# Later squares of the gate weights and a later read of the spread maxima in an attention and GLU kernel

## The chip, the cores and the metric

The kernel runs on one core of one Trainium2 chip. The metric is device time of one execution in microseconds, as the median of the runs shown. TensorE (PE, with its weight loads as PEld), VectorE (DVE), ScalarE (ACT), GpSimd (POOL) and SyncE (SP) work side by side and wait for each other through semaphores. Nearly all transfers are issued by SyncE, in the order in which they are written.

## The reference

A block with a layer norm, sliding-window attention and a gated bilinear feed-forward network, all in float32:

```python
x = A_x                                   # 1 x 2048 x 576
xn = _layernorm(x, axis=-1)
s = _A_ref(xn, A_wqkv, A_wo)              # 32 heads of 18, window 256, softmax
g = _silu(_B_ref(xn, B_w_gate, B_w_up, B_w_down))   # ((xn Wg) * (xn Wu)) Wd, F = 4608
return x + s * g
```

## The kernel before

Every float32 operand is split into two float16 halves, a high and a low one, and a product is made of three float16 matmuls. Weights are first scaled by a power of two, which needs a bound on the size of each weight block.

A prologue normalizes and transposes `x` and projects it to queries, keys and values, which go to DRAM. Then the main loop runs over 72 slots (`NSLOT = NG * NCH`, 18 groups of 256 hidden columns by 4 pieces of the work). One slot makes seven products of the feed-forward network (P1 to P7, a Strassen-like scheme, `prod`) into the PSUM banks `up` and `pv`, and eight accumulations of the down projection (`down`, banks `dn` and `s`). Beside it runs one attention step out of 64, that is two heads and 512 queries: scores into the banks `s` (`score_pairs`), mask and maximum on VectorE (`score`, L982), exponentials on ScalarE (`probs`, L987 and L989), the cast to float16 (`probs_hi`, L994), the low halves on GpSimd (`turn_probs`, L1003), a transposing DMA (L1006), and the product with the values (`weigh`, L1015). Each step has four such rounds, i = 0 to 3.

What the next group needs is made ready one to three slots ahead:

- `ffn_raw` loads the raw weights of gate, up and down.
- `ffn_amax` (L511) takes sums of squares of them on ScalarE, six calls for a group, the last two on the two halves of the gate weights. Its discarded elementwise output goes to the buffer of the tile `spread`, and the sums to `am`.
- `ffn_spread_out` adds the two halves on GpSimd (L515) and writes `am`, 128 x 3 numbers, to DRAM (`sd_f`, L148).
- `ffn_spread_in` reads `sd_f` back so that each partition holds the sums of all 128 (`spread`, L152, 192 KB).
- `ffn_scale` takes their maximum on VectorE (L523) and forms the scales in five tiny instructions on VectorE (L137 to L142) and three on GpSimd (L525 to L527).

The order on each engine comes from one table of times, `W`: `at(slot, t, f, ...)` enters each piece of work at `slot * 18.65 + t`, the list is sorted by that number, and the pieces are issued in that order. Engines then run in order and wait only for data and buffers. The entries of this change are entered with slot `b - 3`, `b` being the first slot of the group, so a time above 18.65 falls in the slot after:

```python
for n in range(6):
    at(b - 3, W["amax"][n], ffn_amax, g, (1, 1, 2, 2, 0, 0)[n], n % 2)
at(b - 3, W["so"], ffn_spread_out, g)
at(b - 3, W["si"], ffn_spread_in, g)
at(b - 2, W["scale"], ffn_scale, g)
```

Neighbours in that slot, on the same scale: the first round's exponentials at 0.77, its cast at 1.85, its low halves and transposition at 2.85, the copy-out `ca1` of product P1 (`copy_out`, L412) at 2.16, the second round's exponentials at 2.98 and its transposition at 5.07, the key loads of the next step at 4.98, its query loads (L952, L953) at 9.2, and `ffn_scale` at 14.98.

Of the kernel before, what the change touches and what calls it, by code (L numbers as in the profile page):

```python
# [20 lines left out]
def kernel(  # L21
# [23 lines left out]
    scale = DH ** -0.5  # L45
# [1003 lines left out]

    NSLOT = NG * NCH  # L1050
    T = 18.65
    W = {"ttr": [-1.39, -1.33, 0.83, 1.5, 8.88, 9.07, 9.1, 9.53], "exp": [0.77, 2.98, 9.73, 10.74], "cast": [1.85, 4.76, 10.51, 10.85], "plo": [2.85, 5.07, 12.24, 14.56], "fin": 5.65, "whi": [7.64, 14.18, 6.44, 16.68], "wlo": [9.45, 16.18, 10.42, 17.34], "dhi": 12.29, "dlo": 17.87, "dlow": 18.11, "sum0": [15.33, 16.23, 24.54], "sum1": [-13.0, 2.34, 7.21], "amax": [12.28, 6.38, 14.78, 15.38, 18.5, 19.95], "scale": 14.98, "hhi0": 18.35, "hlo0": 22.24, "hhi1": 24.39, "hlo1": 26.95, "h1": 18.74, "pv": [17.46, 3.55], "raw0": 10.11, "so": 20.77, "si": 26.88, "pe": {"P5a": 1.05, "P6": 4.39, "P2": 6.57, "P5b": 3.5, "P7": 8.18, "P4": 14.91, "P3": 12.3}, "dn": [1.65, 5.32, 10.61, 10.7, 12.29, 12.31, 16.97, 17.89], "ev": {"ca1": 2.16, "ca2": 6.15, "ca3": 9.47, "add1": 12.5, "add3": 12.36, "t0": 17.27, "add2": 16.63}, "ons": [2, 3, 4, 7], "ld": {"k": 4.98, "q": 9.2, "v": 1.72, "raw1": 1.11, "raw2": 2.66}}
    todo = []

    def at(slot, t, f, *a):
        todo.append((slot * T + t, len(todo), f, a))

    first_slot = 1
    for s in range(NSTEP):
        b = first_slot + s  # L1060
        at(b - 1, W["ld"]["k"], load_k, s)
        at(b - 1, W["ld"]["q"], load_q, s)
        at(b, W["ld"]["v"], load_v, s)
        at(b - 1, 16.6, score_pairs, s, 0)
        at(b, 7.1, score_pairs, s, 2)
        for n in range(8):
            i, j = divmod(n, 2)
            at(b, W["ttr"][n], score, s, i, j)
        for i in range(4):
            at(b, W["exp"][i], probs, s, i)  # L1070
            at(b, W["cast"][i], probs_hi, s, i)
            at(b, W["plo"][i], turn_probs, s, i)
# [272 lines left out]
```

## Time and profile before

| | us |
|---|---|
| median of 3 runs (1571.2 to 1572.65) | 1571.51 |
| profiled execution | 1569.04 |
| its span, first to last instruction | 1567.3 |
| VectorE, all waits for the read of the spread maxima (L523) | 4.3 |
| ScalarE, all squares (L511), 108 calls | 76.8 |

A profile's timeline has a row for each instruction or merged run of instructions: start, duration, engine, line, operation, tiles written and read, shapes, count, and in brackets the idle time of the engine just before it with what ended it. Times count from the start of the span. The waits view sums those idle times by the waiting and the releasing line. A row of the windows view gives, for a stretch, its length, each engine's busy time, the granted clock of TensorE, the mean busy share of the 16 DMA engines and the GB/s moved.

### The profile page before, as it was taken

What the parts mean: (1) busy time and instruction counts of PE and PEld (TensorE: products, weight loads), DVE (VectorE), ACT (ScalarE), POOL (GpSimd) and SP (SyncE); (2) the same over time, 40 slices, a digit from 0 to 9 for tenths busy, and PEclk for the clock granted to TensorE, in tenths of its full rate; (3) what the DMA queues carried; (4) which work ended last, traced back from release to release, by engine and by line L of the source; (5) the groups of instructions that cost most, each with busy time, mean ns of one, the idle gap of its engine ahead of it and who ended that gap; (6) DMA issues with size and microseconds to landing.
All of it is one profiled execution on the core that took longest, in us unless ns stands there. A gap on an engine that the chain in (4) does not pass through costs nothing. (4 is left out here: it accounts for less than half of the span.)

```text
span 1567.3 us, 32521 instructions
## 1 busy us (share of the span) xinstructions
PE 1545.7 (99%) x11857; PEld 890.9 (57%) x11857; DVE 1264.7 (81%) x2914; ACT 1022.1 (65%) x1987; POOL 852.2 (54%) x860
## 2 busy tenths in 40 slices
PE   8999999999999999999999999999999999999998
PEld 5454445555555555555555555555555555555577
DVE  7768678777788989898989888888989898957554
ACT  6547587676767777777777776767777777733230
POOL 3344365646465757576666666575757575822100
PEclk9999999999999999999999999999999999999999
DMA  9593366565748586867777677758686758540435
GB/s 235 165 237 114 113 126 134 103 134 89 143 81 165 109 173 112 156 135 143 136 141 134 132 147 134 156 113 158 116 160 120 160 107 172 98 106 10 98 87 171
DMA packets 556144, 208.68 MB, mean 133 GB/s; under 512 B 492112, under 2 KB 536784, under 8 KB 555984
## 3 DMA queue, kind: packets, MB, share of 16 engines
q1 hardware_dynamic: 555984, 206.60, 63.5%
q8 instruction: 93, 1.52, 0.4%
q14 instruction: 67, 0.55, 0.1%
HBM read 79.25 MB, written 23.75 MB: 66 GB/s over the span
## 5 line engine op out<-in xcount | busy, mean ns | idle before, releaser
L1109 PEld LDWEIGHTS <-hh 128*128 128x128 f16 x3456 | 328.5, 98 | 154.1 <-issue 23.6
L1109 PE MATMUL dn<-dnw,hh 128*128 128x288 f16 x1656 | 248.7, 286 | 0.8 <-DVE acc L1121 0.8
L1109 PE MATMUL s<-dnw,hh 128*128 128x288 f16 x1800 | 243.0, 286 | 2.8 <-DVE mx L982 2.8
L1089 ACT ACTIVATE hh<-ft 128x512 f16<-128x512 f32 x144 | 90.3, 627 | 214.0 <-DVE ft L1081 212.5
L1121 DVE SCALAR_TENSOR_TENSOR acc<-dn,sc,acc 128x288 f32<-128x288 f32 x260 | 133.5, 514 | 112.6 <-PE dn L1109 112.4
L387 PEld LDWEIGHTS <-wg 128*128 128x128 f16 (+1 forms) x1064 | 103.4, 97 | 125.6 <-issue 36.4
L412 ACT ACTIVATE ft<-up 128x512 f32<-128x512 f32 x222 | 130.4, 587 | 66.8 <-PE up L387 65.4
L1121 DVE SCALAR_TENSOR_TENSOR acc<-s,sc,acc 128x288 f32<-128x288 f32 x284 | 141.0, 509 | 19.3 <-PE s L1109 19.0
L542 POOL TENSOR_TENSOR stage<-stage 128x256 f32<-128x256 f32 (+1 forms) x180 | 149.0, 845 | 11.4 <-DVE stage L166 5.8
L387 PE MATMUL pv<-XT,wg 128*128 128x512 f16 x608 | 151.7, 380 | 0.0
L1093 DVE SCALAR_TENSOR_TENSOR hh<-hh,ft 128x512 f16<-128x512 f16 x144 | 143.1, 994 | 2.8 <-ACT hh L1089 2.7
L387 PEld LDWEIGHTS <-ws 128*128 128x128 f16 x988 | 91.2, 97 | 95.0 <-issue 12.4
L387 PEld LDWEIGHTS <-stage 128*128 128x128 f16 x988 | 90.9, 97 | 94.8 <-issue 12.1
L387 PE MATMUL up<-XT,stage 128*128 128x512 f16 (+1 forms) x532 | 139.6, 380 | 0.0
L1085 POOL TENSOR_TENSOR ft<-ft 128x512 f32<-128x512 f32 x72 | 92.0, 1278 | 86.6 <-DVE ft L416 86.6
L387 PE MATMUL up<-XT,ws 128*128 128x512 f16 x504 | 132.2, 380 | 0.0
L416 DVE SCALAR_TENSOR_TENSOR ft<-up,ft 128x512 f32<-128x512 f32 x148 | 101.3, 684 | 33.7 <-PE up L387 24.2
L387 PEld LDWEIGHTS <-wu 128*128 128x128 f16 x760 | 73.6, 97 | 90.9 <-issue 32.2
L387 PE MATMUL up<-TX,stage 128*128 128x512 f16 x456 | 111.1, 379 | 0.6 <-ACT ft L412 0.6
L387 PE MATMUL up<-XT,wg 128*128 128x512 f16 x444 | 107.9, 379 | 3.1 <-DVE ft L416 1.7
L387 PE MATMUL up<-XT,wu 128*128 128x512 f16 (+1 forms) x296 | 108.2, 383 | 0.0
L387 PE MATMUL up<-TX,wu 128*128 128x512 f16 x444 | 107.9, 379 | 0.0
(1265 smaller groups left out, 3125.3 us busy)
## 6 DMA issues: line engine op xcount, KB each, us to landing
stage<-in_B_w_down_dram SPq DMA_DIRECT2D x36, 288.0 KB
stage<-in_B_w_up_dram SPq DMA_DIRECT2D x36, 256.0 KB
stage<-in_B_w_gate_dram SPq DMA_DIRECT2D x36, 256.0 KB
vt<-v_d SPq DMA_DIRECT2D x48, 111.0 KB
ks<-qk_d SPq DMA_DIRECT2D x96, 54.0 KB
xr<-in_A_x_dram SPq DMA_DIRECT2D x16, 288.0 KB
qk_d<-qp SPq DMA_DIRECT2D x18, 256.0 KB
qs<-qk_d SPq DMA_DIRECT2D x128, 36.0 KB
```

The source lines that it names most:

```text
L387: nc.tensor.matmul(ps.rearrange("p (m n) -> p m n", n=128), w, b, start=start, stop=stop, skip_group_check=True)
L412: nc.scalar.activation(FT[sl, name], BK[bk], AF.Copy, scale=by)
L416: nc.vector.scalar_tensor_tensor(f, BK[bk], by, f, op0=OP.mult, op1=OP.add)
L542: nc.gpsimd.tensor_tensor(s_[:, d:d + 2] if d < 8 else s_[:, 8], x_, y_, op=op)
L1085: nc.gpsimd.tensor_tensor(f, f, FT[sl, "a3"], op=OP.mult)
L1089: nc.scalar.activation(hh[:, 0], FT[sl, ("a1", "a2")[c]], AF.Copy, scale=1.0 / LO)
L1093: nc.vector.scalar_tensor_tensor(hh[:, 1], hh[:, 0], -LO, FT[sl, ("a1", "a2")[c]], op0=OP.mult, op1=OP.add)
L1109: nc.tensor.matmul(ps[:, :HALF], a, b, start=n == 0, stop=n == len(l) - 1)
L1121: nc.vector.scalar_tensor_tensor(d, ps[:, :HALF], SC[g][:, 9:10], d, op0=OP.mult, op1=OP.add)
```

## The change

The last two of the six calls of `ffn_amax` move from 18.5 and 19.95 to 19.6 and 21.0, that is to 0.95 and 2.35 of the next slot. The write of the sums moves from 20.77 to 21.9 (3.25) and the read from 26.88 to 28.2 (9.55). It holds for the 17 groups after the first. `W` is one long line; these are its changed entries:

```diff
-"amax": [12.28, 6.38, 14.78, 15.38, 18.5, 19.95]
+"amax": [12.28, 6.38, 14.78, 15.38, 19.6, 21.0]
...
-"so": 20.77, "si": 26.88
+"so": 21.9, "si": 28.2
```

On ScalarE, around the first two rounds of a late step (`spread,am<-stage 128x640` is a square of half of the gate weights, `mx` and `sm` belong to the exponentials, `ft<-up` is `ca1`, `hh` belongs to the down projection), before:

```order
L1089 ACTIVATE hh<-ft 128x512
L511 ACTIVATE spread,am<-stage 128x640
L987 ACTIVATE mx<-mx 128x2
L989 ACTIVATE sm__14571<-sm__14571,mx 128x384 x2
L511 ACTIVATE spread,am<-stage 128x640
L994 CAST pp<-sm__14571 128x2x384
L412 ACTIVATE ft<-up 128x512
L987 ACTIVATE mx<-mx 128x2
```

and now:

```order
L1089 ACTIVATE hh<-ft 128x512
L987 ACTIVATE mx<-mx 128x2
L989 ACTIVATE sm__14571<-sm__14571,mx 128x384 x2
L511 ACTIVATE spread,am<-stage 128x640
L994 CAST pp<-sm__14571 128x2x384
L412 ACTIVATE ft<-up 128x512
L511 ACTIVATE spread,am<-stage 128x640
L987 ACTIVATE mx<-mx 128x2
```

The first square went behind the first exponentials, the second behind the cast and the copy-out. On GpSimd the addition L515 went in the same way from ahead of the first round's low halves to behind them.

On SyncE, the same step (`pt<-pp` are the transpositions of the rounds, `ks` and `qs` the key and query loads), before:

```order
L148 DMA sd_f_14646<-am 128x3
L1006 DMA_TRANSPOSE pt<-pp 128x12x128
L944 DMA ks<-qk_d 36x768
L945 DMA ks<-qk_d 18x768
L944 DMA ks<-qk_d 36x768
L945 DMA ks<-qk_d 18x768
L1006 DMA_TRANSPOSE pt<-pp 128x12x128
L152 DMA spread<-sd_f_14646 128x384
L952 DMA qs<-qk_d 36x512
L953 DMA qs<-qk_d 18x512
L952 DMA qs<-qk_d 36x512
L953 DMA qs<-qk_d 18x512
```

and now:

```order
L1006 DMA_TRANSPOSE pt<-pp 128x12x128
L148 DMA sd_f_14655<-am 128x3
L944 DMA ks<-qk_d 36x768
L945 DMA ks<-qk_d 18x768
L944 DMA ks<-qk_d 36x768
L945 DMA ks<-qk_d 18x768
L1006 DMA_TRANSPOSE pt<-pp 128x12x128
L952 DMA qs<-qk_d 36x512
L953 DMA qs<-qk_d 18x512
L952 DMA qs<-qk_d 36x512
L953 DMA qs<-qk_d 18x512
L152 DMA spread<-sd_f_14655 128x384
```

The write of the sums went behind the first transposition, and the read behind the four query loads. The order of the instructions on TensorE and VectorE is the same.

More of the change, by code (lines that the diff above doesn't have):

```diff
@@ L1051 @@
     T = 18.65
-    W = {"ttr": [-1.39, -1.33, 0.83, 1.5, 8.88, 9.07, 9.1, 9.53], "exp": [0.77, 2.98, 9.73, 10.74], "cast": [1.85, 4.76, 10.51, 10.85], "plo": [2.85, 5.07, 12.24, 14.56], "fin": 5.65, "whi": [7.64, 14.18, 6.44, 16.68], "wlo": [9.45, 16.18, 10.42, 17.34], "dhi": 12.29, "dlo": 17.87, "dlow": 18.11, "sum0": [15.33, 16.23, 24.54], "sum1": [-13.0, 2.34, 7.21], "amax": [12.28, 6.38, 14.78, 15.38, 18.5, 19.95], "scale": 14.98, "hhi0": 18.35, "hlo0": 22.24, "hhi1": 24.39, "hlo1": 26.95, "h1": 18.74, "pv": [17.46, 3.55], "raw0": 10.11, "so": 20.77, "si": 26.88, "pe": {"P5a": 1.05, "P6": 4.39, "P2": 6.57, "P5b": 3.5, "P7": 8.18, "P4": 14.91, "P3": 12.3}, "dn": [1.65, 5.32, 10.61, 10.7, 12.29, 12.31, 16.97, 17.89], "ev": {"ca1": 2.16, "ca2": 6.15, "ca3": 9.47, "add1": 12.5, "add3": 12.36, "t0": 17.27, "add2": 16.63}, "ons": [2, 3, 4, 7], "ld": {"k": 4.98, "q": 9.2, "v": 1.72, "raw1": 1.11, "raw2": 2.66}}
+    W = {"ttr": [-1.39, -1.33, 0.83, 1.5, 8.88, 9.07, 9.1, 9.53], "exp": [0.77, 2.98, 9.73, 10.74], "cast": [1.85, 4.76, 10.51, 10.85], "plo": [2.85, 5.07, 12.24, 14.56], "fin": 5.65, "whi": [7.64, 14.18, 6.44, 16.68], "wlo": [9.45, 16.18, 10.42, 17.34], "dhi": 12.29, "dlo": 17.87, "dlow": 18.11, "sum0": [15.33, 16.23, 24.54], "sum1": [-13.0, 2.34, 7.21], "amax": [12.28, 6.38, 14.78, 15.38, 19.6, 21.0], "scale": 14.98, "hhi0": 18.35, "hlo0": 22.24, "hhi1": 24.39, "hlo1": 26.95, "h1": 18.74, "pv": [17.46, 3.55], "raw0": 10.11, "so": 21.9, "si": 28.2, "pe": {"P5a": 1.05, "P6": 4.39, "P2": 6.57, "P5b": 3.5, "P7": 8.18, "P4": 14.91, "P3": 12.3}, "dn": [1.65, 5.32, 10.61, 10.7, 12.29, 12.31, 16.97, 17.89], "ev": {"ca1": 2.16, "ca2": 6.15, "ca3": 9.47, "add1": 12.5, "add3": 12.36, "t0": 17.27, "add2": 16.63}, "ons": [2, 3, 4, 7], "ld": {"k": 4.98, "q": 9.2, "v": 1.72, "raw1": 1.11, "raw2": 2.66}}
     todo = []
```

## The prediction

> **What bounds the kernel now.** I read the page first, then the waits, then the timelines of the engines around one read of the maxima.
>
> ```profile
> span 1567.3 us, 32521 instructions
> PE 1545.7 (99%) x11857; PEld 890.9 (57%) x11857; DVE 1264.7 (81%) x2914; ACT 1022.1 (65%) x1987; POOL 852.2 (54%) x860
> ```
>
> TensorE is busy 99% of the span, so an edit that gives it no work and takes none away can move the time only through its stalls. The waits view, from 470 to 1400 us, lists them (waiter, releaser, total, times, longest; the last line is the whole span):
>
> ```profile
> PE s L1109 <- DVE mx L982: 2.8, 6, 1.2
> DVE sc L523 <- DMA spread<-sd_f: 2.1, 5, 1.0
> PE up L387 <- ACT ft L412: 0.9, 3, 0.5
> ...
> DVE sc L523 <- DMA spread<-sd_f: 4.3, 6, 2.2
> ```
>
> TensorE's timeline shows what they cost. Product P2 (`pv<-XT,wg`) opens at one fixed place in every step, so its starts are a ruler:
>
> ```profile
> 499.60 0.59 PE L387 MATMUL pv<-XT,wg 128*128 128x512 f16 x2
> ...
> 872.26 0.81 PE L387 MATMUL pv<-XT,wg 128*128 128x512 f16 x3
> ...
> 891.75 1.03 PE L387 MATMUL pv<-XT,wg 128*128 128x512 f16 x4
> ...
> 1022.67 1.99 PE L387 MATMUL pv<-XT,wg 128*128 128x512 f16 x8
> ...
> 1042.66 1.99 PE L387 MATMUL pv<-XT,wg 128*128 128x512 f16 x8
> ...
> 1098.26 1.03 PE L387 MATMUL pv<-XT,wg 128*128 128x512 f16 x4
> ...
> 1116.79 1.03 PE L387 MATMUL pv<-XT,wg 128*128 128x512 f16 x4
> ...
> 1358.75 1.03 PE L387 MATMUL pv<-XT,wg 128*128 128x512 f16 x4
> ```
>
> A step without a stall takes 1116.79 - 1098.26 = 18.53. The 46 steps from the first row to the last take 859.15, against 46 x 18.53 = 852.38: only 6.8 us are lost there. The steps from 872.26 and 1022.67 take 19.49 and 19.99; they are steps that reduce the spread maxima, as is the one of 18.53. On VectorE in these three:
>
> ```profile
> 881.96 0.67 DVE L523 TENSOR_REDUCE sc<-spread 128x3 f32<-128x384 f32 x1 [0.98 <-DMA spread<-sd_f]
> ...
> 883.49 0.17 DVE L142 TENSOR_SCALAR sc<-sc 128x3 f32<-128x3 f32 x1
> ...
> 1031.44 0.68 DVE L523 TENSOR_REDUCE sc<-spread 128x3 f32<-128x384 f32 x1
> 1032.15 1.60 DVE L137 TENSOR_SCALAR sc<-sc 128x3 f32<-128x3 f32 x1
> ...
> 1034.41 0.17 DVE L142 TENSOR_SCALAR sc<-sc 128x3 f32<-128x3 f32 x1
> ...
> 1106.91 0.67 DVE L523 TENSOR_REDUCE sc<-spread 128x3 f32<-128x384 f32 x1
> ...
> 1108.54 0.17 DVE L142 TENSOR_SCALAR sc<-sc 128x3 f32<-128x3 f32 x1
> ```
>
> L142, the chain's last instruction, starts 11.23, 11.74 and 10.28 after the step's ruler; the steps lose 0.96, 1.46 and 0. The differences from 10.28 are 0.95 and 1.46. **So each microsecond by which this chain ends late is a microsecond of TensorE**, through the scores behind it (L982) that free a bank for `down`. There is no slack to lean on.
>
> **The change, part by part.** No instruction is added or removed. Per group two squares, one small addition and two DMAs move. First the squares, on ScalarE and GpSimd, in the group before 1031:
>
> ```profile
> 1016.58 0.72 ACT L511 ACTIVATE spread<-stage 128x640 bf16<-128x640 f32 x1
> 1017.30 0.19 ACT L987 ACTIVATE mx<-mx 128x2 f32<-128x2 f32 x1
> ...
> 1031.18 0.83 ACT L994 CAST pp<-sm__14754 128x768 f16<-128x768 f32 x1 [1.55 <-DMA pt<-pp]
> ...
> 1020.16 2.05 POOL L1003 TENSOR_TENSOR pp<-sm__14571,pp 128x768 f16<-128x768 f32 x1 [0.53 <-ACT pp L994]
> 1022.81 1.64 POOL L1003 TENSOR_TENSOR pp<-sm__14625,pp 128x768 f16<-128x768 f32 x1 [0.60 <-ACT pp L994]
> ...
> 1032.09 1.64 POOL L1003 TENSOR_TENSOR pp<-sm__14754,pp 128x768 f16<-128x768 f32 x1 [1.98 <-ACT pp L994]
> ```
>
> The first square now follows the first exponentials and the second follows the copy-out `ca1`. The exponentials, the first cast, the first GpSimd pass and `ca1` move 0.72 ahead; the second exponentials still have two squares before them and stay. Three times TensorE waited for `ca1` (L412); with 0.72 more room these go: **-0.9** (the waits' own sum; 0 at least, as ScalarE cannot lose there).
>
> Then SyncE's queue:
>
> ```profile
> 1007.56 0.83 SPq L952 DMA_DIRECT2D qs<-qk_d  x1
> ...
> 1009.56 0.40 SPq L158 DMA_DIRECT2D stage<-in_B_w_gate_dram  x1
> ...
> 1019.66 0.34 SPq L148 DMA_DIRECT2D sd_f<-am  x1
> 1022.24 1.45 SPq L1006 DMA_TRANSPOSE pt<-pp  x1
> ...
> 1025.74 1.44 SPq L1006 DMA_TRANSPOSE pt<-pp  x1
> 1027.28 0.83 SPq L152 DMA_DIRECT2D spread<-sd_f  x1
> 1028.16 0.39 SPq L952 DMA_DIRECT2D qs<-qk_d  x1
> ```
>
> Four query loads behind a transposition hold the queue 1009.56 - 1007.56 = 2.00; the read falls behind them. Against that: the first transposition starts when its GpSimd pass ends, 0.72 earlier, or 1.1 if the pass takes 1.64 instead of 2.05; I take 0.9. `sd_f`, so far issued while SyncE was idle, now stands between this transposition and the key loads: 0.4. It meets no wait there: the second square ends near 1020.7, before SyncE arrives near 1022.8. Behind it stand the key loads and the second transposition; the latter's pass is done at 1024.45, 1.29 before it is issued, so it starts 0.9 - 0.4 = 0.5 earlier. The read is therefore issued 2.00 - 0.5 = 1.5 later. The first DMA behind a transposition takes 0.83 to issue, another 0.39: the read gets the short one, so its data can leave 1.5 - 0.44 = 1.06 later. The last part is the transfer:
>
> ```profile
> 1027.00:1028.50 1.50, 1.50 (x15) 1.21 (x13) 1.26 (x5) 1.40 (x3) 0.05 (x1) 1.00 1.11 210
> 1029.00:1031.00 2.00, 2.00 (x14) 1.18 (x12) 1.16 (x4) 0.63 (x2) 1.10 (x1) 1.00 0.56 124
> ```
>
> The column before the last is the DMA share. The second transposition fills the engines (1.11) when the read is issued; the read then runs with the query loads (0.56). In its new place it meets neither a full set of engines nor later loads beside it. I take off another 0.45: **the reduction's data land 0.6 later**. Bounds: 1.5 (no relief) and -0.5 (the read bound by the transposition alone, which starts 0.5 earlier).
>
> Who pays 0.6? The first case is the early group:
>
> ```profile
> 222.34 1.02 PE L387 MATMUL up<-XT,wg 128*128 128x512 f16 x4 [1.51 <-DVE ft L416]
> ...
> 355.57 0.52 SPq L152 DMA_DIRECT2D spread<-sd_f  x1
> ...
> 362.37 0.67 DVE L523 TENSOR_REDUCE sc<-spread 128x3 f32<-128x384 f32 x1
> ```
>
> Six reductions already wait for the data (five in the stretch, and the early one of 2.2, behind which TensorE stood 1.51): they pay in full, 6 x 0.6 = **+3.6**. Three early groups like that of 362.37 have 6.8 between issue and reduction where the later ones have 4.2 (1031.44 - 1027.28): covered by 2.6. Twelve groups lie in the stretch; seven don't wait, of which three are a case of their own, next. The other four have landed just in time; I give them 0.3 of cover, since the waits show that landing scatters by more than that: 4 x 0.3 = **+1.2**.
>
> The three collide with GpSimd. L137 took 1.60 at 1032.15 and ended when GpSimd's pass of 1032.09 did:
>
> ```profile
> L137 DVE TENSOR_SCALAR sc<-sc 128x3 f32<-128x3 f32 x18 | 6.7, 373 | 0.6
> ```
>
> At an undisturbed 0.17 the eighteen would take 3.1; of the 3.6 above it 1.43 are this collision, and I take the rest, 2.2, for two more like it. The pass is late there because its cast waited 1.55 for the second transposition (1031.18). That one is issued 0.5 earlier, so the pass ends up to 0.5 earlier, and a later read is hidden behind it: about **-1.3**. The Trainium skill ("Trainium Architecture — The Big Picture", section "What this means for kernel authors") says that only VectorE's and GpSimd's shared port pair contends, as an exclusive lock. By that rule the trace agrees: the tiny L137 outlasts the pass by 0.02.
>
> Sum: 3.6 + 1.2 - 1.3 - 0.9 = **+2.6 us**. The profiled execution took 1569.04 (span 1567.3 and 1.74 around it), so it would take 1571.6. The median shown is 1571.51, 2.47 above that execution: **1574.1 us**.
>
> **The rivals.** *Full delay (slower).* SyncE's order decides and the transfer gets no relief: data land 1.3 later, six pay 7.8, four pay 1.0 each, the collisions are unchanged: 7.8 + 4.0 - 0.9 = +10.9, 1582.4. It decides once the delay passes 0.9 (six times that, four times 0.6, less 2.2: +5.6). For it: 2.00 us of queue are certain. Against: the full engines until 1028.5. The Trainium skill ("DMA: Bandwidth & Descriptors", "Queues, rings and completion order") speaks for it: on each DMA engine descriptors are consumed in ring order, so the read waits for all four loads' data. By that rule none of the 0.45 that I took off is sure. The shares above can't separate the two.
>
> *The read comes no later (same).* The 1.06 are made up by idle DMA engines. Then only ScalarE's 0.9 and the collisions' 1.3 remain: -2.2, 1569.3.
>
> *The read lands earlier (faster).* If the second transposition's drain alone sets it, data land 0.5 earlier; of 2.1 waited in the stretch some 1.7 go, 0.5 in the early group, 1.3 and 0.9 as above: -4.4, 1567.1. For it: the share of 1.11 just ahead of the read. Against: the read can't be issued before the loads.
>
> *The squares don't free `ca1`*: then 0.9 stays and the forecast becomes 1575.0. L412 waits 0.9 in all, so this can't be more; it is counted inside the forecast's own spread.
>
> **How the numbers follow.** Forecast 0.45, full delay 0.25, no later 0.18, earlier 0.12. About 0.2% (3.1 us, from 1568.4 to 1574.7) is what a measurement of this kernel can tell from no change. The forecast lies at that edge, with 2 us of its own to each side (1572 to 1576): 0.19 of its 0.45 count as slower. Slower: 0.19 + 0.24 = 0.43. Faster: 0.10 of the earlier landing and 0.04 of the no-later case: 0.14. The same: 0.43. The range 1568.5 to 1582.5 leaves out most of the earlier landing and the upper part of the full delay.
>
> **What would show it.** On SyncE the read starts some 1.5 later against the ruler, the second transposition 0.5 earlier. L523 waits for `spread<-sd_f` in nine or more steps instead of six, in total about 4.3 + 4.8 = 9 us if I am right, 16 under full delay, under 4 if it lands earlier. `PE up <- ACT ft` in the stretch goes to nothing, `PE s <- DVE mx` grows from 2.8 to about 6. L137's mean falls from 373 ns. L142 minus the ruler, less 10.28, still gives each step's loss; if a step loses time with L142 on schedule, my model of the bound is wrong. I am wrong too if the query loads' data hold the read for longer than their issue does, or if the fourth GpSimd pass moves onto the chain in steps that were free of it.

## The result and the profile after

| | before | after |
| --- | --- | --- |
| median, us (6 runs each, same chip) | 1571.36 (1570.29 to 1572.65) | 1576.17 (1575.31 to 1579.59) |
| ratio, 95% interval | | 1.0037 (1.0026 to 1.0048) |
| profiled execution, us (span) | 1569.04 (1567.3) | 1575.93 (1574.2) |

The changed kernel is slower by 4.8 us in the medians and by 6.9 in the profiled executions. The page after shows the same work in a longer span:

```profile
span 1574.2 us, 32493 instructions
PE 1546.0 (98%) x11857; PEld 891.0 (57%) x11857; DVE 1266.0 (80%) x2914; ACT 1021.8 (65%) x1987; POOL 851.4 (54%) x860
```

TensorE's busy time has grown by 0.3 us (1545.7 before), so the 6.9 are stalls. The waits view, 470 to 1400 us (waiter, releaser, total, times, longest), and in the last line the same wait over the whole span:

```profile
DVE sc L523 <- DMA spread<-sd_f: 13.0, 12, 2.0
ACT pp L994 <- DMA pt<-pp: 10.6, 12, 1.8
PE s L1109 <- DVE mx L982: 9.7, 10, 1.6
...
DVE sc L523 <- DMA spread<-sd_f: 15.2, 13, 2.2
```

All twelve reductions of the stretch now wait for their data, 13.0 us in all where five waited 2.1, and TensorE's wait for the scores behind them has gone from 2.8 to 9.7. TensorE's wait for `ca1` (`PE up <- ACT ft`) has no row any more in this stretch. TensorE's timeline gives the ruler, the starts of P2:

```profile
499.58 1.03 PE L387 MATMUL pv<-XT,wg 128*128 128x512 f16 x4
...
951.71 1.03 PE L387 MATMUL pv<-XT,wg 128*128 128x512 f16 x4
...
972.24 1.03 PE L387 MATMUL pv<-XT,wg 128*128 128x512 f16 x4
...
1027.84 1.03 PE L387 MATMUL pv<-XT,wg 128*128 128x512 f16 x4
...
1046.89 1.03 PE L387 MATMUL pv<-XT,wg 128*128 128x512 f16 x4
...
1365.64 1.03 PE L387 MATMUL pv<-XT,wg 128*128 128x512 f16 x4
```

The 46 steps take 866.06, 13.7 more than 46 undisturbed ones (852.38); before they lost 6.8. The difference, 6.9, is the whole difference of the two profiled executions. Two reducing steps show what is in it: the one from 1027.84 loses 19.05 - 18.53 = 0.52, the one from 951.71 loses 2.00. SyncE in the first:

```profile
1026.30 1.28 SPq L1006 DMA_TRANSPOSE pt<-pp  x1
1027.67 0.99 SPq L148 DMA_DIRECT2D sd_f<-am  x1
1028.71 0.41 SPq L944 DMA_DIRECT2D ks<-qk_d  x1
...
1030.30 1.45 SPq L1006 DMA_TRANSPOSE pt<-pp  x1
1031.80 0.84 SPq L952 DMA_DIRECT2D qs<-qk_d  x1
...
1033.77 0.35 SPq L152 DMA_DIRECT2D spread<-sd_f  x1
```

Against the ruler, the first transposition is issued at -1.54 (before: 1022.24 - 1022.67 = -0.43), the second at 2.46 (before 3.07) and the read at 5.93 (before 4.61). So the queue did what the prediction said: second transposition 0.6 earlier, read 1.3 later. This step is the mildest case. Over the twelve reducing steps of the stretch the read is issued 5.93 to 6.93 after the ruler, 6.30 on average, against 4.73 on average before, and the end of its issue moves from 5.57 to 6.75. VectorE in the two steps, first 951.71, then 1027.84:

```profile
962.45 0.68 DVE L523 TENSOR_REDUCE sc<-spread 128x3 f32<-128x384 f32 x1 [2.00 <-DMA spread<-sd_f]
...
963.98 0.17 DVE L142 TENSOR_SCALAR sc<-sc 128x3 f32<-128x3 f32 x1
...
1037.11 0.66 DVE L523 TENSOR_REDUCE sc<-spread 128x3 f32<-128x384 f32 x1 [0.54 <-DMA spread<-sd_f]
...
1038.64 0.17 DVE L142 TENSOR_SCALAR sc<-sc 128x3 f32<-128x3 f32 x1
```

In the second of them the data come 0.54 late, close to the 0.6 of the forecast. In the first they come 2.00 late. L142 minus the ruler, less 10.28, is 1.99 and 0.52, the steps' losses again. Most of the difference already stands in SyncE's queue. In the step from 951.71:

```profile
955.73 0.84 SPq L952 DMA_DIRECT2D qs<-qk_d  x1
...
958.00 1.51 SPq L152 DMA_DIRECT2D spread<-sd_f  x1
```

The issue of the read starts 6.29 after the ruler and lasts 1.51 instead of 0.35, so it ends at 7.80 where the other step has 6.28. That is 1.52 later, against a difference of 1.47 in L142. The order of the transfers is the same in both steps; what differs is what the DMA engines move. The windows of the step from 951.71 (the last two columns are the DMA share and GB/s; the share books a packet's whole time to the window in which it starts, so it can pass 1), and behind the dots those of the step from 1027.84, from 2.6 after its ruler:

```profile
953.51:954.31 0.80, 0.80 (x8) 0.31 (x5) 0.80 (x2) 0.54 (x1) 0.72 (x2) 1.00 0.66 92
954.31:955.11 0.80, 0.80 (x6) 0.34 (x4) 0.80 (x5) 0.06 (x1) 0.45 (x1) 1.00 1.66 35
955.11:955.91 0.80, 0.80 (x8) 0.56 (x7) 0.80 (x5) 0.71 (x2) 0.00 (x0) 1.00 0.24 27
955.91:956.71 0.80, 0.80 (x9) 0.65 (x7) 0.80 (x3) 0.72 (x3) 0.00 (x0) 1.00 0.68 72
...
1030.44:1031.24 0.80, 0.80 (x6) 0.35 (x4) 0.80 (x5) 0.06 (x1) 0.44 (x1) 1.00 0.03 10
1031.24:1032.04 0.80, 0.80 (x8) 0.56 (x7) 0.80 (x5) 0.72 (x2) 0.00 (x0) 1.00 0.25 35
1032.04:1032.84 0.80, 0.80 (x9) 0.65 (x7) 0.79 (x3) 0.72 (x3) 0.00 (x0) 1.00 0.93 180
```

For some 2.4 us behind the write of the sums, while key loads and the second transposition are under way, the engines move 27 to 72 GB/s. The other step is as slow for 1.6 us, but then reaches 180; a second transposition that runs freely has the engines at some 210 (the window of 1027.00 in the prediction). I call it a **standstill** when, between 1.5 before and 4 after the issue of the second transposition, at least four packets of the trace are open at once that each stay open for more than 1 us. Counted so, eight of the twelve reducing steps have one after the change. They lose 0.94 to 2.00, and their read's issue ends 6.61 to 7.80 after the ruler. The other four lose 0.22 to 0.52, and their read's issue ends at 6.28 to 6.36. Before the change three steps had one. That the standstill is what holds SyncE's issues is plausible but not shown.

### The profile page after: what moved, and what is told of

The parts are those of the page before. It is cut to its first block, busy times and chain, and to the rows that moved or that the text cites. A ratio compares the mean times of both kernels' runs of the same rounds, so it can differ in the third digit from the quotient of the medians.

```text
span 1574.2 us, 32493 instructions
## 1 busy us (share of the span) xinstructions
PE 1546.0 (98%) x11857; PEld 891.0 (57%) x11857; DVE 1266.0 (80%) x2914; ACT 1021.8 (65%) x1987; POOL 851.4 (54%) x860
## 3 DMA queue, kind: packets, MB, share of 16 engines
q8 instruction: 93, 1.52, 0.4%
## 5 line engine op out<-in xcount | busy, mean ns | idle before, releaser
L412 ACT ACTIVATE ft<-up 128x512 f32<-128x512 f32 x222 | 130.3, 587 | 66.2 <-PE up L387 64.9
L1093 DVE SCALAR_TENSOR_TENSOR hh<-hh,ft 128x512 f16<-128x512 f16 x144 | 155.0, 1077 | 3.1 <-ACT hh L1089 3.1
L387 PEld LDWEIGHTS <-ws 128*128 128x128 f16 x988 | 90.9, 97 | 93.9 <-issue 11.2
```

The source lines that it names most:

```text
L387: nc.tensor.matmul(ps.rearrange("p (m n) -> p m n", n=128), w, b, start=start, stop=stop, skip_group_check=True)
L412: nc.scalar.activation(FT[sl, name], BK[bk], AF.Copy, scale=by)
L1093: nc.vector.scalar_tensor_tensor(hh[:, 1], hh[:, 0], -LO, FT[sl, ("a1", "a2")[c]], op0=OP.mult, op1=OP.add)
```

## The experiments

"Lost" is what 46 steps take above 852.38, from the first and last ruler row of each profile; ratios are against runs of the kernel before on the same chip (medians 1569.4 for the first four rows, 1568.91 for the copy on chip, the 1 x 3 write and the last two, 1570.25 for the others).

| run | median, us | ratio (95%) | ruler, first and last | lost |
| --- | --- | --- | --- | --- |
| squares and write, not the read | 1571.19 | 1.0009 (1.0000 to 1.0018) | 499.01, 1361.07 | 9.7 |
| read alone | 1587.42 | 1.0117 (1.0103 to 1.0131) | 502.04, 1376.99 | 22.6 |
| write alone | 1587.06 | 1.0114 (1.0100 to 1.0128) | 500.39, 1379.69 | 26.9 |
| all three, write behind the keys | 1582.36 | 1.0084 (1.0069 to 1.0100) | 498.75, 1370.94 | 19.8 |
| all three, write issued by ScalarE | 1573.88 | 1.0031 (1.0018 to 1.0044) | 500.63, 1364.16 | 11.2 |
| before, extra DRAM write of 128 x 3 | 1592.07 | 1.0138 (1.0125 to 1.0151) | 502.84, 1382.16 | 26.9 |
| before, extra DRAM load of 128 x 3 | 1575.14 | 1.0028 (1.0015 to 1.0041) | 500.57, 1366.47 | 13.5 |
| before, extra on-chip copy of 128 x 3 | 1576.05 | 1.0042 (1.0029 to 1.0055) | 500.81, 1365.80 | 12.6 |
| before, extra DRAM write of 1 x 3 | 1570.42 | 1.0008 (0.9999 to 1.0018) | 499.95, 1360.07 | 7.7 |
| before, read ahead of the keys | 1573.15 | 1.0017 (1.0008 to 1.0026) | 499.09, 1363.66 | 12.2 |
| squares, write by ScalarE, not the read | 1567.47 | 0.9990 (0.9981 to 0.9998) | 498.42, 1358.36 | 7.6 |
| before, read ahead of the keys, chain earlier | 1564.89 | 0.9973 (0.9962 to 0.9985) | 500.08, 1354.63 | 2.2 |

### Taking the change apart

**Squares and write without the read.**

```diff
 (changed kernel)
-"si": 28.2
+"si": 26.88
```

> The squares and the write of the sums stand as in the change; the read of the maxima is back ahead of the query loads. Queue theory (the read comes late because it is issued behind the query loads): the read is issued near 4.0 us after the ruler instead of 5.9, its waits on VectorE fall from 13.0 in the stretch to about 2 or less, and 1568 to 1571 us result. Hold-up theory (the write, now directly ahead of the key loads, holds up the DMA engines, and with them the second transposition and the read behind it): the transposition still drains no earlier than before the change and in some steps up to 1 us later, the waits stay at 4 or more, 1571 to 1574 us.

The read is issued about 4.0 after the ruler in eight of the twelve steps. In the four others SyncE waits for the write of the sums to land, and the read goes out at 5.1 to 7.6. Seven of twelve reductions do not wait, the others 4.3 in all, and nine steps still have a standstill. The time lies in the hold-up theory's range. 1.0009 for this and 1.0037 for the whole change make the read's move worth 0.28% here, 4.4 us; what is left, squares and write together, costs 1.4 us, just at the edge of its interval, where the forecast had a gain.

**The read alone.**

```diff
 (kernel before)
-"si": 26.88
+"si": 28.2
```

> Only the read moves behind the query loads; the squares and the write stand as before the change. Queue theory: the read is issued 2.0 us later than before, the waits exceed 15 in the stretch, slower than the whole change: 1578 to 1582 us. Hold-up theory: the delay is that of the queue alone, about 1 us at the landing and evenly spread over the steps, without single steps that lose 2 us: 1576 to 1580 us. If both parts share the loss, it comes out below the whole change, 1572 to 1576.

The waits of this run, 470 to 1400 us:

```profile
DVE sc L523 <- DMA spread<-sd_f: 18.5, 12, 2.4
PE s L1109 <- DVE mx L982: 16.5, 12, 2.2
```

With nothing else moved the read is issued 6.5 after the ruler, 1.9 later than before, and the waits grow by 18.5 - 2.1 = 16.4, or 1.37 for each of the twelve. All of a delay is paid except 0.56, not much more than the 0.44 of the shorter issue: of the further 0.45 that I took off for emptier DMA engines little is left. Standstills are nearly as rare as before (four steps), so this is mostly queue delay. Two steps lost about 4, more than this accounts for, and the time lies above both theories' ranges.

**The write alone.**

```diff
 (kernel before)
-"so": 20.77
+"so": 21.9
```

> Only the write of the sums moves, to behind the first transposition; the squares and the read stand as before the change. Queue theory: the key loads, the second transposition and the read are issued 0.4 us later, the six waiting steps pay 0.4 each: about +2.5, 1573 to 1575 us. Hold-up theory: as in the whole change the DMA engines stand still for about 1 us near the second transposition in most of the twelve steps, which adds to the 0.4: 1575 to 1579 us.

The write, so far issued while SyncE was idle, now stands between the first transposition and the key loads. That is 0.4 us of queue by my sum, and it costs 1.14%, again more than either theory had. The second transposition is issued 3.58 after the ruler instead of 3.07, the read at 5.1 when nothing more holds it. That is so in five of the twelve steps; in the others it goes out at 6.2 to 8.0. In two of these the second transposition takes over 3 us to issue. In the other five SyncE waits for the write: the read of the sums cannot start before they are in DRAM, and here it stands only 4 us behind their write. SyncE's waits, 470 to 1400 us:

```profile
SPq L152 <- DMA sd_f<-am: 10.7, 5, 2.9
```

Before, the write stood 7.6 ahead of the read, and no reducing step of the stretch had this wait; in the changed kernel, where the read stands 6 behind it, none has it either. So part of the 1.14% is that dependence, which neither theory had. L523 waits 17.3 in all, but ScalarE also waits 22.9 for transpositions (6.9 before) and TensorE's scores 9.3 for the queries. Ten of twelve steps have a standstill.

The write alone and the read alone cost some 18 us each, and all three edits together about 5. The later squares let the first transposition go at -1.54 instead of -0.43, and with it the rest of the queue. Beside the moved write they are worth 15.9 us (1587.06 against 1571.19), so they pay for most of what the other two do. Later squares by themselves were not tried: the write where it stood would wait on SyncE, ahead of that transposition, for sums that come later.

### What about the write costs so much

**Write behind the key loads.**

```diff
 (changed kernel)
-"so": 21.9
+"so": 23.65
```

> The whole change, but the write of the sums stands behind the key loads, directly ahead of the second transposition. Queue theory: the number of DMAs ahead of the read is the same, nothing changes, 1576 us. Hold-up theory, if it is the key loads that wait behind the write: the standstills near the second transposition go or get rarer, the steps that lose 1.9 and 2.0 us fall under 1.0, 1572 to 1574 us.

Slower than the changed kernel, not faster, so both theories missed. Standstills are fewer (three steps) but last over 2 us, and in these steps the first query load takes 2.5 to 2.7 us to issue instead of some 0.8. L523 waits 16.5. The cost does not go away with the place ahead of the keys; why the few are longer is not explained.

**Four small transfers in the write's new place.** To the kernel before, one transfer per group was added whose data nothing uses, in the order of the table behind the first transposition and ahead of the key loads:

```diff
+    def tiny_dma(g):
+        TW[g] = dram.tile([128, 3], F32, name=f"tw{g}")
+        nc.sync.dma_start(TW[g], sig[:, 0:3])
...
+            at(b - 3, 21.9, tiny_dma, g)
```

> The kernel before, with one more DMA per group: 1.5 KB of constants to DRAM, unused afterwards, at the place in SyncE's queue that the write of the sums has in the change (behind the first transposition, ahead of the key loads). It costs the queue 0.4 to 0.5 us. Queue theory: the read is issued that much later and six to ten steps pay it, 3 to 5 us slower than before. Hold-up theory (a small write to DRAM directly ahead of the key loads brings the DMA engines to a standstill near the second transposition): 9 or so of the twelve steps show it, 10 to 18 us slower than before, as with the write alone moved.

For the load the transfer is

```diff
+        nc.sync.dma_start(tiny, x[0:128, 0:3])
```

> As the run with the extra write, but the extra DMA at that place is a load of 1.5 KB from DRAM to SBUF, unused afterwards. Queue theory: the same as the extra write, 3 to 5 us slower. Hold-up theory: no more standstills than before the change, so also 3 to 5 us slower, and at least 6 us less than the extra write. If both extra DMAs are alike and over 8 us slower, it is the place in the queue and not the write that counts.

for the on-chip copy

```diff
+        nc.sync.dma_start(tiny, sig[:, 0:3])
```

> Before, with one extra copy of 128 x 3 numbers from on-chip memory to on-chip memory in the same place. If the DRAM as the target makes the cost: 1573 to 1577, as the load from DRAM. If reading on-chip memory in 128 small pieces makes it: 1585 to 1595, as the write.

and for the short write

```diff
+        TW[g] = dram.tile([1, 3], F32, name=f"tw{g}")
+        nc.sync.dma_start(TW[g], sig[0:1, 0:3])
```

> Before, with one extra DRAM write of only 3 numbers from one partition, in the place where the write of 128 x 3 numbers cost 1.38% and a load of the same size 0.28%. If any DRAM write there holds the queue up until it is received: 1585 to 1595, standstills of the DMA engines near the second transposition in 8 or more of the 12 reducing steps. If it is the 128 small pieces of the write, spread over all DMA engines: 1573 to 1577, as the load, with standstills in 2 to 4.

All four hold the same place in the queue, and cost 1.38%, 0.28%, 0.42% and 0.08%. The place in the queue is therefore cheap; 128 pieces cost 0.3 to 0.4% wherever they go, and 128 pieces into DRAM a further 1%. A DRAM write of one piece does not cost that; it has fewer bytes as well, so pieces and bytes are not told apart. The write cost more than the 10 to 18 us that I had for it, and the one-piece write less than either of my two ranges. Nothing depends on these transfers, so a read that waits for its write, as with the write alone, cannot be the cause here. The same 3.2 us of one step, from 3.4 after its ruler (806.55 with the write, 800.29 with the load), in the windows view, first the write:

```profile
809.95:810.75 0.80, 0.80 (x8) 0.56 (x7) 0.80 (x4) 0.73 (x3) 0.00 (x0) 1.00 1.78 33
810.75:811.55 0.80, 0.80 (x9) 0.65 (x7) 0.79 (x3) 0.72 (x3) 0.00 (x0) 1.00 0.07 14
811.55:812.35 0.80, 0.80 (x9) 0.63 (x8) 0.58 (x3) 0.80 (x2) 0.02 (x1) 1.00 1.74 70
812.35:813.15 0.80, 0.80 (x6) 0.36 (x4) 0.80 (x2) 0.77 (x3) 0.80 (x1) 1.00 0.19 23
```

and the load:

```profile
803.69:804.49 0.80, 0.80 (x8) 0.56 (x7) 0.80 (x4) 0.73 (x3) 0.00 (x0) 1.00 0.43 121
804.49:805.29 0.80, 0.80 (x9) 0.65 (x7) 0.78 (x3) 0.72 (x3) 0.00 (x0) 1.00 0.36 81
805.29:806.09 0.80, 0.80 (x9) 0.63 (x8) 0.58 (x3) 0.80 (x2) 0.02 (x1) 1.00 1.13 213
806.09:806.89 0.80, 0.80 (x6) 0.36 (x4) 0.80 (x2) 0.77 (x3) 0.80 (x1) 1.00 1.14 213
```

TensorE's columns are the same to the digit; what differs are the DMA columns: 14 to 70 GB/s behind the write, 81 to 213 behind the load. Near the second transposition the write's profile has standstills in eleven of twelve steps, the three others in two or three each. What waits in the write's profile, 470 to 1400 us (lines are 6 higher there, L1000 is L994):

```profile
ACT pp L1000 <- DMA pt<-pp: 27.0, 14, 3.2
...
DVE sc L529 <- DMA spread<-sd_f: 15.2, 12, 2.0
```

It is all that comes through these engines, the transpositions first. The Trainium skill ("DMA: Bandwidth & Descriptors", section "Anatomy of one DMA — SWDGE (gpsimd) path") puts most of the fixed cost of a DMA issued through GpSimd down to the receipt from the target memory, with DRAM the heaviest. By that rule the runs agree in direction, 1.38% into DRAM against 0.42% on chip, though SyncE issues these and nothing waits for them; but the one-piece write, into DRAM too, costs 0.08%, so the target alone does not make the cost.

**The write issued by ScalarE.**

```diff
 (changed kernel)
-    def spread_out(key, am, n):
+    def spread_out(key, am, n, by=None):
...
-        nc.sync.dma_start(SD[key], am)
+        (by or nc.sync).dma_start(SD[key], am)
...
-        spread_out(f"f{g}", am[:, 0], 3)
+        spread_out(f"f{g}", am[:, 0], 3, nc.scalar if g else None)
```

> The whole change, but the write of the sums is issued by ScalarE, behind its second exponentials, and not by SyncE. Queue theory: SyncE's queue is 0.9 us shorter ahead of the read, six to twelve steps gain 0.5 to 0.9 each: 4 to 6 us faster than the change, near the time before. Hold-up theory: the same gain at least, and the standstills near the second transposition go: at or under the time before.

1.0031 beside 1.0037: no difference that the intervals can tell, where I had expected 4 to 6 us of gain. Standstills fall to seven steps and the read's waits to 9.5, but GpSimd's pass, whose cast stands behind that issue on ScalarE, now has 17.4 us of idle time put down to issue in twelve steps.

### Whether the chain or its collisions set the end

**Read ahead of the keys.**

```diff
 (kernel before)
-"si": 26.88
+"si": 23.55
```

> The kernel before, with the read of the maxima moved ahead of the key loads instead of behind the query loads. Both theories: it lands 3 us earlier, the waits for it on VectorE (2.1 in the stretch) go. The second transposition is issued 0.5 to 0.9 later, so that the fourth pass on GpSimd may meet the scale chain in more steps. If landing is all that counts: 3 to 4 us faster than before. If the collisions take its place: no faster, with a mean of L137 well above 373 ns.

No reduction waits for data any more, and the kernel is still slower. L137 and L139 collide with GpSimd's pass instead:

```profile
L137 DVE TENSOR_SCALAR sc<-sc 128x3 f32<-128x3 f32 x18 | 8.9, 496 | 0.6
L139 DVE TENSOR_SCALAR sc<-sc 128x3 int32<-128x3 int32 x18 | 5.9, 328 | 0.6
```

At 169 ns each they would take 6.1 together; they take 14.8. The chain now starts 8.65 after the ruler in every step. GpSimd's pass waits for ScalarE's cast, and the cast waits longer for transpositions, 17.6 against 6.9 before. So the pass starts 8.3 to 10.3 after the ruler and overlaps the chain in all twelve steps.

**The same with the chain earlier.**

```diff
 (kernel before)
-"si": 26.88
+"si": 23.55
-"scale": 14.98
+"scale": 13.05
```

> Before, with the read ahead of the key loads and the reduction with its chain moved ahead of one copy-out of the down projection (7.4 instead of 8.65 after the ruler), so that the chain ends before GpSimd's last pass starts at 9.5. If the collisions with GpSimd are what the early read alone still paid (L137 and L139 up to 1.64 in 8 of 12): these go to 0.17 each, 46 steps lose under 6, 1566 to 1569. If the later copy-out or the later transpositions set it: 1572 or more, with waits of TensorE for L1121 or of ScalarE for the transposed data as large as before (17.6).

The reduction now stands ahead of one copy-out of the down projection. One step of it, on TensorE, SyncE, VectorE and GpSimd:

```profile
1021.03 1.03 PE L387 MATMUL pv<-XT,wg 128*128 128x512 f16 x4
...
1021.89 0.84 SPq L152 DMA_DIRECT2D spread<-sd_f  x1
...
1028.32 0.67 DVE L523 TENSOR_REDUCE sc<-spread 128x3 f32<-128x384 f32 x1
1029.02 0.17 DVE L137 TENSOR_SCALAR sc<-sc 128x3 f32<-128x3 f32 x1
...
1029.84 0.17 DVE L142 TENSOR_SCALAR sc<-sc 128x3 f32<-128x3 f32 x1
...
1030.09 0.19 POOL L525 TENSOR_TENSOR sc<-sc 128x1 f32<-128x1 f32 x1 [1.62 <-DVE sc L142]
...
1030.75 1.65 POOL L1003 TENSOR_TENSOR pp<-sm__14754,pp 128x768 f16<-128x768 f32 x1
```

L142 starts 8.81 after the ruler and GpSimd's pass 9.72. This is more than the chain being early. `ffn_scale` also has three instructions on GpSimd (L525 to L527). Its new time, 13.05, puts them ahead of the pass (14.56) in GpSimd's order, and L525 waits for L142, so the pass can no longer start while the chain runs. In the twelve reducing steps it starts at 9.7 or later, behind a chain that ends near 9.0. The earlier reduction and the new order on GpSimd were not tried apart. Over the eighteen groups neither instruction is stretched:

```profile
L139 DVE TENSOR_SCALAR sc<-sc 128x3 int32<-128x3 int32 x18 | 3.0, 169 | 0.6
L137 DVE TENSOR_SCALAR sc<-sc 128x3 f32<-128x3 f32 x18 | 3.0, 169 | 0.6
```

and 46 steps lose 2.2 in place of 12.2; I had expected under 6. This version is faster than both kernels, 0.9973 (0.9962 to 0.9985), although ScalarE still waits 13.1 for transpositions.

**The write on ScalarE and the read where it was.**

```diff
 (changed kernel with the write issued by ScalarE)
-"si": 28.2
+"si": 26.88
```

> The changed kernel with the sums' write issued by ScalarE (as in the run at 1573.9) and the read back in front of the queries' loads. If the read's later place is what that run still paid: read near 4.2 after the ruler, reductions wait under 4 in all, 1569 to 1571. If the ScalarE issue itself costs (GpSimd idle for issue 17.4 there): 1572 to 1575.

0.9990 (0.9981 to 0.9998), just ahead of the kernel before: the reductions wait 1.2 in all. With the write on ScalarE the read's later place costs 0.41%, with the write on SyncE 0.28%. So in both forms the read's move is what makes the change a loss.

## Why the prediction was right or wrong

The forecast, slower by 2.6 us at 1574.1, had the sign and the path of the delay; the measured 4.8 (medians) lies inside the range and below the full delay. The size was a good deal too small, and that the time came out only 2.1 above the forecast is partly luck: the medians differ by less than the two profiled executions, and one gain was twice what I had. By terms, against the profiled 6.9:

- **The bound** held. Each step's loss is still L142's lateness, 1.99 and 0.52 in the two steps above and to 0.01 in all twelve, and the 46 steps account for all 6.9.
- **ScalarE, -0.9**: right. TensorE's waits for L412 are gone from the stretch.
- **The queue** was right on average: the read is issued 1.57 later (forecast 1.5), 1.3 in the step shown, and the second transposition 0.6 earlier (0.5). Two errors cancel in this: the first transposition came 1.1 earlier instead of 0.9, and the write holds the queue 1.04 (1027.67 to 1028.71; about 0.9 in most steps) instead of 0.4, as the first transfer behind a transposition, of which the key load behind it, now a short one, gives back some 0.4.
- **The collisions, -1.3**: right in direction, but less than half of what was measured. L137's mean fell from 373 to 218 ns, 2.8 us in all:

```profile
L137 DVE TENSOR_SCALAR sc<-sc 128x3 f32<-128x3 f32 x18 | 3.9, 218 | 0.6
```

- **The landing, 0.6 later, for +3.6 and +1.2**: this is the step that was mis-sized. The stretch's waits grew by 13.0 - 2.1 = 10.9 where I had 4.2. That is 0.91 a step on average. The delay was larger, and all twelve reductions wait, where I had five pay in full, four pay half and three nothing. (The early group, for which I had 0.6, paid nothing: 2.2 before and after.) I priced the write at its queue time and gave every group the same 0.6. The four steps without a standstill wait 0.23 to 0.54, within the forecast; the eight others wait 0.88 to 2.00. The sum with what was measured is 10.9 - 2.8 - 0.9 = 7.2, close to the 6.9.
- **The relief of 0.45** for emptier engines came out at about half. From the end of the read's issue to the reduction it takes 3.06 on average after the change, and 3.30 in the five steps that waited before: 0.24. The read alone had 0.56 of relief in all, of which the shorter issue gives 0.44.

Of the rivals, full delay is refuted as a time (1582.4), but its waits were the better forecast. They would have grown by 7.8 + 4.0 = 11.8, against a measured 10.9. L523 waits 15.2 in all, where I had named 16 as the sign of full delay and 9 as that of my own. Its time was not reached mainly because the collisions, which it left as they were, fell by 2.8. The read landing no later or earlier is refuted by twelve waiting reductions.

A mechanism I did not list adds to the waits: a small write into DRAM ahead of loads and a transposition slows the DMA engines. That it does so is shown by the four small transfers. That it explains all of the extra wait in the changed kernel is argued: the standstills lie in the steps that lose most, but moving the write behind the keys or to ScalarE did not bring the time back. Which property of the 128 pieces does it also stays open.

## What to carry to other kernels

Price a DMA that is moved by what it does to the transfers behind it and by what waits for it to land, not only by its issue time: in this kernel a DRAM write in many small pieces belongs where nothing urgent follows, and well ahead of the read that needs it. Where a reduction is just in time, an earlier load is worth nothing until its consumer moves as well, out of the way of the other engine that it collides with; moving both gave 4 us where moving the load alone lost 2.9. Ask what else a new time reorders: here it also put the consumer's part on GpSimd ahead of the pass that collided. Edits that each cost 18 us alone may cost 5 together, so a change in several parts has to be taken apart in pairs too.

## What the runs showed of the hardware that was not expected

- An extra 1.5 KB write into DRAM per group, in 128 pieces, cost 21.8 us over the kernel (1592.07 against 1570.25), a load of the same size in the same place 4.9, and a 12-byte write in one piece 1.5 (its interval takes in no change).
- While the rate is low the DMA share tells nothing of it: beside the extra write it is 1.78 with 33 GB/s and 0.07 with 14. A high share alone does not say that data move.
- The 1.5 KB write of the sums was slow to land itself. In the nine reducing steps in which SyncE waited for it (four with squares and write moved, five with the write alone), the read went out 4.2 to 6.9 us after the write's issue.
- A 0.17 us VectorE instruction was held for up to 1.64 us next to a GpSimd pass, L139 as well as L137. The Trainium skill ("Trainium Architecture — The Big Picture", section "What this means for kernel authors") has the shared port as an exclusive lock; by that rule the trace agrees, 14.8 us for two lines that take 6.0 when the pass does not overlap.
